# A grouped 1x1 convolution that streams through SBUF: input and output rings of four slots each, in place of three and five

## The chip, the core and the metric

The kernel runs on one core of a Trainium2 chip. The core has five engines, each with its own instruction queue: TensorE (PE, matrix products; its weight loads are listed as PEld), VectorE (DVE), ScalarE (ACT), GpSimd (POOL) and SyncE (SP). They are synchronised by semaphores only. Sixteen DMA engines move data between the memory (HBM) and the on-chip buffer (SBUF, 128 partitions); matrix products land in PSUM. Transfers are issued here by SP, ACT and GpSimd, and each of the three has its own DMA queue on every DMA engine.

The metric is the device time of one execution in microseconds (us), the median over several runs. A profile is one further execution with an instruction and DMA trace; its times are its own.

## The reference

The input `x` is 1 x 512 x 512 x 192 in bf16, the weights `w` are 1 x 1 x 4 x 48 x 48. The 192 channels of each pixel form four groups of 48, and each group is multiplied by its own 48 x 48 matrix:

```
xg  = x.reshape(B, H, W, 4, 48)
out = einsum('bhwgc,gcd->bhwgd', xg, w[0, 0]).reshape(B, H, W, 192)
```

There are 262,144 pixels of 384 bytes: 100.66 MB to read and as much to write.

## The kernel before

**Pieces and slots.** The pixels are cut into pieces (`plan_pieces`, L78). A full piece has 64 columns (`SLOT`): 128 partitions, each with 64 consecutive pixels, 24,576 bytes per partition and 3.1 MB in all. There are 34 slots in order, numbered from 0. Slot 0 is loaded as three pieces of 8, 24 and 32 columns (`HEAD`). Slots 6 and 22 (`SHARED_AT`) are shared ones: they hold data in part of the partitions only, partitions 0 to 15 with 48 columns, moved by SP's queue (by ACT's when stored), and partitions 52 to 95 with 64 columns, moved by GpSimd's queue. With them the DMA engines get unequal shares. The last slot has 8 columns.

**Rings.** `xin` and `xout` are rings in SBUF. The input ring has `IN_COLS` = 192 columns, three slots; the output ring has `OUT_COLS` = 320 columns, five slots. A slot's place in a ring is its column modulo the ring's size.

**Groups and pairs.** Four columns make a group (16 groups in a slot), two groups a pair. For each pair PE transposes twelve 128 x 128 blocks of `xin` into PSUM (`transposes`, L260), DVE copies them to SBUF as bf16 (`evacuate`, L311), PE multiplies the twelve blocks by a banded weight matrix `wt` (`matmuls`, L275), and ACT copies each group's result from PSUM to `xout` (L345). PE works one pair ahead with the transposes.

**Loops.** PE's code is a loop whose body is as long as the input ring: `LOOP` = `IN_COLS // 4` = 48 groups, `LP` = 24 pairs. There are 265 pairs: 11 turns of the loop and one pair behind it. DVE loops over the same number of pairs. ACT, SP and GpSimd have straight code.

**What sets the order.** Each engine's list is written out by hand.
- SP (L228) waits before each load until the slot's room in the ring is free (`groups_before`, L179: PE has transposed the slot that was there before), and then issues the load.
- GpSimd (L184) goes through the pieces. For each it first looks at the piece after it; if that is a shared one, it waits for the room and issues GpSimd's part of that load. Then it waits until piece `p` has landed and raises `ready` (L218), on which PE waits. After that it issues GpSimd's part of a shared store, if the piece before was a shared one. Small dummy transfers (`cur`, L203) turn the round-robin over the DMA engines to the wanted one.
- ACT (L323) waits before a group's copy until the store of the slot that was in that place of the output ring has landed (`wait_stored`, L333), then for PE, then copies. A slot's store is issued after the second group of the next slot (L346). The last eight full slots are stored in halves of 32 columns, and the very last of them in four parts (`LATE`, `LAST_PARTS`).

Of the kernel before, what the change touches and what calls it, by code (L numbers as in the profile page):

```python
# [22 lines left out]
ECOLS = 272  # L23

SLOT = 64
IN_COLS = 3 * SLOT
OUT_COLS = 5 * SLOT
HEAD = (8, 24, 32)
LATE = 9
LAST_PARTS = (24, 16, 12, 12)  # L30
LOOP = IN_COLS // 4
SHARED_AT = (6, 22)
SYNC, POOL = 0, 1
SHARED = ((0, 16, 4, 48, SYNC), (52, 44, 11, SLOT, POOL))
NXP = 4
NXS = 2
NOB = 4
# [22 lines left out]
class Piece:  # L60

    def __init__(self, i, slot, g0, size, shares, pix):
        self.i, self.slot, self.size = i, slot, size
        self.at = {IN_COLS: 4 * g0 % IN_COLS, OUT_COLS: 4 * g0 % OUT_COLS}
        self.g0, self.g1 = g0, g0 + size // 4
# [12 lines left out]
def plan_pieces(npix):  # L78
    few = sum(rows * cols for _, rows, _, cols, _ in SHARED)
    at = list(SHARED_AT)  # L80
    if npix < len(at) * few + 128 * SLOT * (1 + at[-1]):
        at = []
    cols = (npix - few * len(at)) // 128
    assert cols % 4 == 0
    pieces, g, pix, n = [], 0, 0, 0
    while cols:
        if n in at:
            parts = [(SLOT, SHARED)]
        elif n == 0 and cols >= SLOT:
            parts = [(s, None) for s in HEAD]  # L90
        else:
            parts = [(min(SLOT, cols), None)]
        for s, shares in parts:
            pieces.append(Piece(len(pieces), n, g, s, shares, pix))
            cols -= 0 if shares else s
            g, pix = pieces[-1].g1, pieces[-1].pix_end
        n += 1
    assert pix == npix
    return pieces


def bass_standalone__grouped__vision_kernel(nc, x, w, out):
# [5 lines left out]
    pieces = plan_pieces(npix)  # L108
# [11 lines left out]
    def groups(pair):  # L120
        return range(2 * pair, min(2 * pair + 2, NG))

    def transfers(ap, ring, p, queue, c0=0, c1=None):
        at = p.at[ring.shape[1] // C]
        for b in p.on(queue):
            px = ap[b.pix:b.pix + b.rows * b.cols, :]
            e0, e1 = c0, min(c1 or b.cols, b.cols)
            if b.parts == 1:
                view = px.rearrange("(p i) n -> p (i n)", p=b.rows)[:, e0 * C:e1 * C]
            else:  # L130
                view = px.rearrange("(c a i) n -> a c (i n)", a=b.parts, c=b.rows // b.parts)
            yield b, view, ring[b.r0:b.r0 + b.rows, (at + e0) * C:(at + e1) * C]

    stores = []
    for p in pieces:
# [6 lines left out]
        for n in parts:  # L142
            stores.append((p, c, c + n, p.g0 + (c + n) // 4))
            c += n
    store_of = {g: i for i, (p, c0, _, g1) in enumerate(stores) for g in range(p.g0 + c0 // 4, g1)}
    pooled = [p for p in pieces if p.on(POOL)]
    pool_val = {p: 16 * len(p.on(POOL)) for p in pooled}

    with ExitStack() as es:
        block = es.enter_context(nc.Block())  # L150
        xin = es.enter_context(nc.sbuf_tensor("xin", [128, IN_COLS * C], BF16))
        xout = es.enter_context(nc.sbuf_tensor("xout", [128, OUT_COLS * C], BF16))
        xT_sb = [es.enter_context(nc.sbuf_tensor(f"xT_sb{i}", [128, 4 * UC], BF16)) for i in range(NXS)]
# [3 lines left out]
        wt = es.enter_context(nc.sbuf_tensor("wt", [128, WCOLS], BF16))  # L157
        xT_ps = es.enter_context(nc.psum_tensor("xT_ps", [128, NXP, 1024], BF16))
        o_ps = es.enter_context(nc.psum_tensor("o_ps", [128, NOB, 512], F32))
# [19 lines left out]
        def groups_before(p):  # L179
            pairs = (p.g1 - LOOP + 1) // 2  # L180
            return max(2 * pairs - 3, pairs > 0)

        @block.gpsimd
        def _(gp):  # L184
            wq = Waiter(gp)
            gp.memset(esel[:], 1.0).then_inc(p0_sem, 1)  # L186
            gp.memset(ident[:], 1.0).then_inc(p1_sem, 1)  # L187
            gp.wait_ge(p0_sem, 1)
            gp.affine_select(out=esel[:], in_=esel[:], pattern=[[-1, ECOLS]],  # L189
                             compare_op=AluOpType.is_equal, fill=0.0, base=ESHIFT,  # L190
                             channel_multiplier=1).then_inc(e_sem, 1)
            gp.wait_ge(p1_sem, 1)
            gp.affine_select(out=ident[:], in_=ident[:], pattern=[[-1, 128]],  # L193
                             compare_op=AluOpType.is_equal, fill=0.0, base=0,
                             channel_multiplier=1).then_inc(id_sem, 1)
            cursor, turns = [0], [0]

            def pool_dmas(p, ap, ring, inward, done):
                for b, dram, sbuf in transfers(ap, ring, p, POOL):
                    turn = (b.engine - cursor[0]) % 16  # L200
                    if turn:
                        few = xf[0:turn, 0:128].rearrange("p (a b) -> p a b", a=2)[:, :, 0:32]
                        gp.dma_start(cur[0:turn, turns[0]], few).then_inc(cur_sem, 16)  # L203
                        turns[0] += 1
                    gp.dma_start(*((sbuf, dram) if inward else (dram, sbuf))).then_inc(done, 16)  # L205
                    cursor[0] = (b.engine + b.parts) % 16

            for p in pieces:
                ahead = pieces[p.i + 1] if p.i + 1 < len(pieces) else None
                if ahead in pooled:  # L210
                    wq.wait(mm_done, groups_before(ahead))
                    pool_dmas(ahead, xf, xin, True, pl_sem[ahead])
                wq.wait(ld_sem[p.i], 16 * len(p.on(SYNC)))
                if p in pooled:
                    wq.wait(pl_sem[p], pool_val[p])
                pairs = (NP if p is pieces[-1] else p.g1 // 2) - p.g0 // 2
                if pairs:
                    gp.sem_inc(ready, pairs)  # L218
                if p.i and pieces[p.i - 1] in pooled:
                    q = pieces[p.i - 1]  # L220
                    wq.wait(mm_done, q.g1 + 2)
                    pool_dmas(q, of, xout, False, ps_sem[q])
            for p in pooled:
                wq.wait(ps_sem[p], pool_val[p])
            wq.wait(cur_sem, 16 * turns[0])

        @block.sync
        def _(sp):  # L228
            wq = Waiter(sp)
            sp.dma_start(w_sb[:], wv).then_inc(w_sem, 16)  # L230
            for p in pieces:
                wq.wait(mm_done, groups_before(p))
                for _, dram, sbuf in transfers(xf, xin, p, SYNC):
                    sp.dma_start(sbuf, dram).then_inc(ld_sem[p.i], 16)  # L234

        @block.tensor
        def _(pe):
# [12 lines left out]
            def transposes(j, gs):  # L250
# [4 lines left out]
                for g in gs:  # L255
                    xg = columns(xin, g)
                    for ul in range(2):
                        for tc in range(3):
                            i = ul * 3 + tc
                            last = pe.transpose(xT_ps[:, g % NXP, i * 128:(i + 1) * 128],  # L260
                                                xg[:, i * 128:(i + 1) * 128], ident[:])
# [40 lines left out]
        def _(dve):  # L302
# [4 lines left out]
            def evacuate(pair, j):  # L307
                n = len(groups(pair))
                b0 = pair * 2 % NXP
                dve.wait_ge(t_left, j + 1)  # L310
# [12 lines left out]
        def _(act):  # L323
# [3 lines left out]
            def store():  # L327
                i = len(stores) - len(todo)
                p, c0, c1, g1 = todo.pop(0)
                for _, dram, sbuf in transfers(of, xout, p, SYNC, c0, c1):  # L330
                    act.dma_start(dram, sbuf).then_inc(st_sem[i], 16)  # L331

            def wait_stored(i):  # L333
                p = stores[i][0]
                wq.wait(st_sem[i], 16 * len(p.on(SYNC)))
                if p in pooled:
                    wq.wait(ps_sem[p], pool_val[p])

            for g in range(NG):
                if g >= OUT_COLS // 4:  # L340
                    wait_stored(store_of[g - OUT_COLS // 4])
                wq.wait(mm_done, g + 1)
# [38 lines left out]
```

## Time and profile before

| | us |
|---|---|
| median of three runs (480.93 to 483.29) | 481.1 |
| profiled execution | 480.09 |
| its span, first to last instruction | 478.35 |
| PE busy | 439.6 |
| ACT busy | 399.1 |
| DVE busy | 254.4 |

The profile counts 201.48 MB over the DMA queues, a mean of 421 GB/s over the span: SP's queue (loads, q1) takes 48.5% of the sixteen DMA engines' time, ACT's queue (stores, q10) 48.4%, GpSimd's (q0) 2.1%. The granted clock of TensorE was full except for 6.8 us from 310.1 us on.

How to read it: an engine's busy share is a mean over the whole span, and a wait is put down to the instruction that released it. "POOLq L218" is GpSimd's forwarding of a landed load, so a wait of PE for it is a wait for a load. "DMA share" is the mean busy share of the sixteen DMA engines in a stretch. A transfer's time to landing runs from its issue to the last of its parts.

### The profile page before, as it was taken

To read this page: it belongs to the slowest core of one execution; us is meant where nothing else is said; L and a number is where in the kernel's file an instruction comes from. 1 tells how busy PE (TensorE), PEld (TensorE's weight loads), DVE (VectorE), ACT (ScalarE), POOL (GpSimd) and SP (SyncE) were. 2 spreads that over 40 slices of the span, in tenths; PEclk is the share of its full clock that TensorE was granted. 3 is DMA by queue.
4 is the path that set the end of the run, shared out by engine and by line. 5 is a ranking of instruction groups with operands and counts; after the bars stand their busy time and mean duration, and the time that the engine had idled before them with its cause. 6 is when DMAs were issued, how large, how long until landed. Compare 5 with 4: busy or idle time off the path is not lost.

```text
span 478.4 us, 14098 instructions
## 1 busy us (share of the span) xinstructions
PE 439.6 (92%) x6370; PEld 395.4 (83%) x6370; DVE 254.4 (53%) x266; ACT 399.1 (83%) x531; POOL 5.9 (1%) x16
## 2 busy tenths in 40 slices
PE   5999999999999998888998888799999999999990
PEld 5989888889888897777887777788889889888880
DVE  2565555555555555545555454356555555555640
ACT  2899899899899987887978878499899989989990
POOL 1000010000000000000000000000000000000000
PEclk9999999999999999999999999799999999999996
DMA  8999999999999999999999999999999999999995
GB/s 330 427 405 438 427 430 417 427 430 438 427 434 430 430 432 432 432 430 436 432 428 430 434 432 433 435 430 423 430 418 427 428 430 424 424 418 422 429 426 247
DMA packets 11978, 201.48 MB, mean 421 GB/s; under 512 B 1744, under 2 KB 1744, under 8 KB 2640
## 3 DMA queue, kind: packets, MB, share of 16 engines
q1 hardware_dynamic: 5144, 98.52, 48.5%
q10 hardware_dynamic: 6376, 98.50, 48.4%
q0 software_dynamic: 448, 4.33, 2.1%
q8 instruction: 5, 0.08, 0.1%
q14 instruction: 5, 0.04, 0.0%
HBM read 100.68 MB, written 100.66 MB: 421 GB/s over the span
## 4 chain that ended last, share of the span: by engine, by line
PE 69%; DMA 27%; issue 1%; ACT 0%; SPq 0%; ACTq 0%; POOLq 0%
PE o_ps L275 40%; PE xT_ps L260 29%; DMA xin<-in_x_dram 27%; ACT xout L345 0%; SPq L234 0%; SPq L230 0%; POOLq L218 0%; ACTq L331 0%; ACTq L50 0%
## 5 line engine op out<-in xcount | busy, mean ns | idle before, releaser
L345 ACT CAST xout<-o_ps 128x768 bf16<-128x768 f32 x530 | 397.8, 802 | 67.1 <-PE o_ps L275 56.3
L311 DVE COPY xT_sb<-xT_ps 128x1536 bf16<-128x1536 bf16 x265 | 253.8, 958 | 206.6 <-PE xT_ps L260 206.6
L275 PE MATMUL o_ps<-wt,xT_sb 128*128 128x144 bf16 (+1 forms) x3180 | 296.3, 235 | 3.5 <-ACT xout L345 0.4
L275 PEld LDWEIGHTS o_ps<-wt,xT_sb 128*128 128x128 bf16 x3180 | 214.7, 98 | 43.8 <-ACT xout L345 29.8
L260 PE MATMUL xT_ps<-ident,xin 128*128 128x128 bf16 x3180 | 224.1, 221 | 20.1 <-POOLq L218 18.6
L260 PEld LDWEIGHTS xT_ps<-ident,xin 128*128 128x128 bf16 x3180 | 192.4, 99 | 23.7 <-POOLq L218 21.0
L203 POOL DMA_DIRECT2D cur<-in_x_dram x4 | 2.3, 584 | 328.3 <-DMA xin<-in_x_dram 178.9
L246 PE MATMUL o_ps<-w_sb,esel 48*128 48x48 bf16 x10 | 0.6, 210 | 2.8 <-DMA w_sb<-in_w_dram 2.8
L246 PEld LDWEIGHTS o_ps<-w_sb,esel 48*128 48x128 bf16 x10 | 0.5, 113 | 2.8 <-issue 2.8
L305 DVE CAST wt<-o_ps 128x480 bf16<-128x480 f32 x1 | 0.7, 657 | 3.4 <-PE o_ps L246 3.4
L345 ACT ACT_TABLE_LOAD x1 | 1.3, 1283 | 0.8 <-PEq L366 0.8
L205 POOL DMA_DIRECT2D xin<-in_x_dram x2 | 1.1, 563 | 0.0
L205 POOL DMA_DIRECT2D out_dram<-xout x2 | 1.1, 560 | 0.0
L189 POOL TENSOR_SCALAR_AFFINE_SELECT esel<-esel 48x272 bf16<-48x272 bf16 x1 | 0.4, 402 | 0.0
L186 POOL MEMSET esel<- 48x272 bf16 x1 | 0.3, 318 | 0.3 <-POOLq L366 0.3
L193 POOL TENSOR_SCALAR_AFFINE_SELECT ident<-ident 128x128 bf16<-128x128 bf16 x1 | 0.3, 282 | 0.0
L187 POOL MEMSET ident<- 128x128 bf16 x1 | 0.2, 198 | 0.0
L366 POOL MEMSET const-float32-0.0<- 128x1 f32 x1 | 0.1, 98 | 0.3 <-issue 0.3
L366 POOL MEMSET const-bfloat16-1.0<- 128x1 bf16 x1 | 0.1, 101 | 0.0
L366 POOL MEMSET const-uint8-127<- 128x1 uint8 x1 | 0.1, 101 | 0.0
L366 POOL MEMSET const-float32-1.0<- 128x1 f32 x1 | 0.1, 99 | 0.0
## 6 DMA issues: line engine op xcount, KB each, us to landing
xin<-in_x_dram SPq DMA_DIRECT2D x30, 3072.0 KB, 22.2
out_dram<-xout ACTq DMA_DIRECT2D x22, 3072.0 KB, 25.1
out_dram<-xout ACTq DMA_DIRECT2D x15, 1536.0 KB, 27.5
out_dram<-xout ACTq DMA_DIRECT2D x2, 1152.0 KB, 16.7
xin<-in_x_dram POOLq DMA_DIRECT2D x2, 1056.0 KB, 15.9
out_dram<-xout POOLq DMA_DIRECT2D x2, 1056.0 KB, 16.3
xin<-in_x_dram SPq DMA_DIRECT2D x1, 1536.0 KB, 8.9
xin<-in_x_dram SPq DMA_DIRECT2D x1, 1152.0 KB, 5.7
```

The lines of the kernel that those rows point to most:

```text
L186: gp.memset(esel[:], 1.0).then_inc(p0_sem, 1)
L189: gp.affine_select(out=esel[:], in_=esel[:], pattern=[[-1, ECOLS]], compare_op=AluOpType.is_equal, fill=0.0, base=ESHIFT, channel_multipli ...
L193: gp.affine_select(out=ident[:], in_=ident[:], pattern=[[-1, 128]], compare_op=AluOpType.is_equal, fill=0.0, base=0, channel_multiplier=1) ...
L203: gp.dma_start(cur[0:turn, turns[0]], few).then_inc(cur_sem, 16)
L205: gp.dma_start(*((sbuf, dram) if inward else (dram, sbuf))).then_inc(done, 16)
L246: last = pe.matmul(o_ps[:, NOB - 1, col:col + CG], lhsT=esel[:, s0:s0 + 128], rhs=w_sb[:, g, :], start=True, stop=True, skip_group_check=True)
L260: last = pe.transpose(xT_ps[:, g % NXP, i * 128:(i + 1) * 128], xg[:, i * 128:(i + 1) * 128], ident[:])
L275: last = pe.matmul(o_ps[:, v % NOB, c0_:c1_], lhsT=xs[:, i * 128:(i + 1) * 128], rhs=wt[:, WOFF[tc]:WOFF[tc] + (c1_ - c0_)], start=(tc == ...
L305: dve.tensor_copy(wt[:], o_ps[:, NOB - 1, 0:WCOLS]).then_inc(wc_sem, 1)
L311: dve.tensor_copy(xT_sb[pair % NXS][:, 0:n * 2 * UC].rearrange("p (g c) -> p g c", g=n), xT_ps[:, b0:b0 + n, 0:2 * UC]).then_inc(e_left, 1)
L345: act.copy(dst, o_ps[:, v % NOB:v % NOB + 2, 0:UC]).then_inc(o_left, 1)
L366: nc = _bacc.Bacc("TRN2", target_bir_lowering=False, num_devices=1)
```

## The change

Both rings get 256 columns, four slots each; together they take the same room as before. Since PE's and DVE's loops are as long as the input ring, their bodies grow from 24 to 32 pairs: 8 turns, and nine pairs behind them. A load of slot k may be issued once slot k-4 is done; ACT's copy into slot k waits for the store of slot k-4. In its list GpSimd looks two pieces ahead for a shared load, not one: a new constant, `AHEAD`, is the number of input slots less two.

```diff
 SLOT = 64
-IN_COLS = 3 * SLOT
-OUT_COLS = 5 * SLOT
+IN_COLS = 4 * SLOT
+OUT_COLS = 4 * SLOT
 HEAD = (8, 24, 32)
...
 SHARED = ((0, 16, 4, 48, SYNC), (52, 44, 11, SLOT, POOL))
+AHEAD = IN_COLS // SLOT - 2
...
             for p in pieces:
-                ahead = pieces[p.i + 1] if p.i + 1 < len(pieces) else None
+                ahead = pieces[p.i + AHEAD] if p.i + AHEAD < len(pieces) else None
                 if ahead in pooled:
                     wq.wait(mm_done, groups_before(ahead))
                     pool_dmas(ahead, xf, xin, True, pl_sem[ahead])
```

## The prediction

> **What bounds the kernel now.** I read the share of each engine first, then the stages, then the waits, then the DMA issues, and last the end of the time line. Page and stages (columns: stretch, its length, then busy time and count for PE, PEld, DVE, ACT, POOL, then clock, DMA share, GB/s):
>
> ```profile
> span 478.4 us, 14098 instructions
> PE 439.6 (92%) x6370; PEld 395.4 (83%) x6370; DVE 254.4 (53%) x266; ACT 399.1 (83%) x531; POOL 5.9 (1%) x16
> PE 69%; DMA 27%; issue 1%; ACT 0%; SPq 0%; ACTq 0%; POOLq 0%
> q8 instruction: 5, 0.08, 0.1%
> ...
> 12.00:60.00 48.00, 47.63 (x698) 42.97 (x696) 27.65 (x29) 43.26 (x58) 0.00 (x0) 1.00 1.01 424
> 76.00:140.00 64.00, 63.04 (x927) 56.59 (x925) 36.77 (x39) 57.61 (x77) 1.10 (x2) 1.00 1.00 429
> 166.00:296.00 130.00, 118.62 (x1730) 105.84 (x1728) 68.86 (x73) 107.84 (x145) 1.10 (x2) 1.00 1.00 432
> 366.00:445.00 79.00, 77.66 (x1146) 70.07 (x1144) 45.75 (x48) 71.41 (x96) 0.00 (x0) 1.00 1.00 425
> 445.00:470.00 25.00, 20.41 (x295) 17.95 (x292) 11.49 (x12) 20.11 (x27) 0.00 (x0) 1.00 1.00 425
> 470.00:478.40 8.40, 0.00 (x0) 0.00 (x0) 0.00 (x0) 0.00 (x0) 0.00 (x0) 0.51 0.42 174
> ```
>
> The chain names PE, but see the DMA share: 1.00 in every stage from 12 to 470 us. All sixteen DMA engines work without a gap, in both directions, and 201.48 MB at 432 GB/s is 466 us by itself. PE is second: it is idle only in the stretch 166 to 296 (118.6 of 130), where it waits for loads. The next lines are the waits, the DMA issues and the end of the time line:
>
> ```profile
> ACT xout L345 <- PE o_ps L275: 56.3, 131, 7.7
> PE xT_ps L260 <- POOLq L218: 18.6, 12, 4.9
> ...
> xin<-in_x_dram SPq DMA_DIRECT2D x30, 3072.0 KB, 22.2
> out_dram<-xout ACTq DMA_DIRECT2D x22, 3072.0 KB, 25.1
> out_dram<-xout ACTq DMA_DIRECT2D x15, 1536.0 KB, 27.5
> ...
> DMA to landing us min/median/max: 10.8/24.6/35.4
> ...
> 301.79 1.46 PE L260 MATMUL xT_ps<-ident,xin 128*128 128x128 bf16 x12 [4.87 <-POOLq L218]
> 466.18 0.80 ACT L345 CAST xout<-o_ps 128x768 bf16<-128x768 f32 x1
> 467.01 0.68 ACTq L331 DMA_DIRECT2D out_dram<-xout  x1
> ```
>
> "PE <- POOLq L218" is PE waiting for a load (GpSimd forwards each landing): 18.6 us in all. ACT never waits for a store, so five output slots are not all needed. The last line is the key to the end: the last store is issued at 467.0, and its sixteen parts land between 472.5 and 477.85. PE and ACT are done 10.8 us before the end; what ends the run is the queue of stores, and in it the most loaded of the sixteen engines.
>
> **The change, part by part.** The sum is made against the profiled execution: 480.09 us, of which 478.35 is the span and 1.74 lies around it. The median of the runs shown, 481.1, is 1.0 above that.
>
> *Loads one slot further ahead.* SP issues the load of slot k when PE has finished slot k-4, not k-3, about one slot (13.1 us at PE's own pace, 14.55 us from 180 to 282, by the spacing of SP's issues) earlier. This gives work to an engine only if its load queue would be empty. From the issue and landing times, transfer by transfer, that is so in one place of weight: slot 5 lands from 65.1 us on, slot 7 is issued at 73.5, and slot 6 is the shared one, so for about 9 us most engines had stores alone. Elsewhere the next load is issued before the last has landed, but for at most 3 us (slot 23 from 313.9, slot 24 issued 316.6). In those gaps the engines were not idle: they worked on stores (share 1.00). The loads so gained cost as much store work. Saving in DMA time: 0. Gain for PE: at equal turns 4.5 us of work moved puts later loads up to 9 us earlier and later stores up to 9 us later; for engines that also had the shared slot in between it is less. I take 6.
>
> *Output ring of four slots.* A whole slot's store is issued after the second group of the next slot and its room is needed at slot k+4's first group: 46 groups of 0.82 us (13.1/16) = 37.7 us, where it was 62 groups, 50.8 us. Half-slot stores near the end have 54 groups, 44.3 us. Landing takes 28.2 us (median from 166 to 296) and 35.4 at most. With stores 6 us later, and issued earlier because PE is earlier, ACT will now wait for stores. Behind that wait on ACT stand its copies and the issue of later stores; PE waits for the copies through four PSUM buffers. What is late next can be read off absolute times: slot 20 begins now when its load lands, at 283.6. In the changed kernel it needs that load (277 to 281) and the store of slot 16 (272.2 now, 278 to 281 then). So PE starts slot 20 some 3 us earlier, held by a store in place of a load. PE's idle time falls from 18.6 us to about 15, between 0 and 34 (bounds: no wait at all; the slowest engine's store pace of 15.1 us per slot, 242.04 to 257.18 to 272.24, holding PE for slots 16 to 33: 17 x 2.0 us). On the path: 0, because DMA keeps its queues filled and PE ends before the stores do.
>
> *GpSimd two pieces ahead.* Its load of slot 6 goes out when slot 2 is done (47.0 us; now 61.4), that of slot 22 when slot 18 is done (about 267; now 284.8). Each sits before GpSimd's release of the slot then due: slot 4 lands at 51.7 and PE needs it at 60.5; slot 20 lands about 280. Neither release is late. Each puts a third queue beside two, four packets of 0.91 us on each of eleven engines. Now that collides with slot 21's load (34.4 us to landing, the longest) and makes the 4.9 us wait at 301.8; the clock is halved for 6.8 us from 310.1 behind it. Moved one slot, it collides with slot 20's instead, or is absorbed. PE idle -8 to +5 us; off the path, 0. SP's own share of the slot moves alike, and GpSimd's cursor DMAs stay four.
>
> *A longer loop.* PE's loop has 32 pairs, not 24; one turn is 1181 instructions in the trace and will be about 1575; 8 turns and 9 pairs behind them. A turn of the loop costs PE some 0.3 us (the 0.2 to 0.5 us before L260 marked issue), so three fewer save 1 us, off the path. Code: five packets of 16 KB, at 17 to 52 us, all in the first turn and each on another engine, 0.94 us each; the longer code needs two to four more. Take 3 x 0.94 / 16 = 0.2 us; bounds 0 and 2.8 (all on the engine that ends last).
>
> *DMA rate.* Stages ran at 424 to 432 GB/s. If the 130 us at 432 fell to 425, +2.1; if the 152 us from 318 to 470 rose to 432, -2.5. No reason for either: 0.
>
> *The end.* With loads ahead, they finish earlier (now 444) and a longer stretch is stores alone. At that point PE still has some 35 us of work and the engines some 45 us of stores (7.3 us per slot: 8 packets of 0.912), so they don't run dry. The last engine's total of bytes is unchanged: 0.
>
> Sum: 480.09 + 0.2 = 480.3; on the median's scale 481.3.
>
> **The rivals.**
> *Slower: the store wait outgrows the reserve behind PE.* Place: ACT's wait for a store before its copy. PE may lose 10.8 - 3.4 = 7.4 us net (3.4 us: the first 384 KB load, the nearest row for a last transfer that meets no queue) before the end moves; then each us costs one. If the pace of 15.1 held from slot 12 to 31, idle is 19 x 2.0 = 38, less the 18.6 and 3.4 us (half of 6.8) of now: +16. Then 467 + 16 + 3.4 = 486.4 span, 489. Against: when PE is held, loads are held too, and the stores catch up. 0.16.
>
> *Slower: the loop's code no longer stays on chip.* A miss at each branch back: 0.94 us behind two packets of 0.91, 2.8 us, 7 times: 19 us; PE at 486, span 490, time 492. For: the body grows by a third. [...] 0.05.
>
> *Slower: DMA works less evenly.* The last engine falls another 2 us behind and the rate falls by the 2.1 us above: 485. 0.09.
>
> *Faster: the load wait was the bound.* A deeper ring takes away the 18.6 us: 462. Against: share 1.00; the bytes alone need 466. 0.02. [...]
>
> *Faster: the engines end closer together.* The mean of the sixteen last landings is 474.0, the last is 477.85. Closing most of it, with the later rate at 432: 476 to 477. 0.16.
>
> **How the numbers follow.** About 0.5% (2.4 us) is what a measurement of this kernel can tell. My case, no change, 0.52, its own range 479 to 483.5. Slower 0.16 + 0.05 + 0.09 = 0.30; faster 0.18. The range 477 to 488 leaves out half of the first slow rival and the second, the 462, and part of the even ending: nearly 2 in 10.
>
> **What would show it.** Right: DMA share 1.00 from 12 to 470; "ACT xout <- DMA out_dram" waits appear, 5 to 15 us in all; PE's waits for L218 fall below 10; seven to nine code packets; last copy at 461 to 470. Wrong: a DMA share under 0.97 in any stage between, a last copy after 475, or code packets in every turn.

## The result: 0.7% faster

Nine runs of the changed kernel have a median of 477.42 us, nine of the kernel before 481.1. The ratio of the means is 0.993, with a 95% interval of 0.9902 to 0.9959. The profiled execution took 477.15 us, its span is 475.2, 3.1 us less than before. The time lies just inside the range that was given (477 to 488), but the forecast was "no change", at 481.3, with 0.18 for faster. It came closest to the last of the rivals: "the engines end closer together", 476 to 477.

The page of the changed kernel, and its stages (columns as in the prediction):

```profile
span 475.2 us, 14075 instructions
PE 437.6 (92%) x6370; PEld 394.6 (83%) x6370; DVE 254.5 (54%) x266; ACT 399.0 (84%) x531; POOL 5.9 (1%) x16
PE 75%; DMA 20%; issue 1%; ACT 0%; SPq 0%; ACTq 0%; POOLq 0%
q8 instruction: 8, 0.13, 0.1%
...
12.00:60.00 48.00, 47.47 (x707) 43.04 (x705) 27.84 (x30) 44.12 (x60) 1.26 (x2) 1.00 1.01 422
76.00:140.00 64.00, 63.11 (x934) 57.06 (x931) 37.05 (x40) 58.32 (x78) 1.11 (x2) 1.00 1.00 431
166.00:296.00 130.00, 118.70 (x1705) 106.66 (x1703) 67.99 (x71) 106.58 (x143) 1.11 (x2) 0.97 1.01 432
366.00:445.00 79.00, 77.79 (x1147) 70.08 (x1145) 45.44 (x48) 71.91 (x96) 0.00 (x0) 1.00 1.00 428
445.00:470.00 25.00, 13.61 (x194) 11.80 (x191) 7.66 (x8) 13.55 (x19) 0.00 (x0) 0.81 0.99 419
470.00:475.20 5.20, 0.00 (x0) 0.00 (x0) 0.00 (x0) 0.00 (x0) 0.00 (x0) 0.50 0.43 177
```

The DMA share is 1.00 again, up to the last stretches. The rate is not the same: 431 for 429 GB/s from 76 to 140, 428 for 425 from 366 to 445. A share of 1.00 says that a packet is under way all the time, not that packets take their usual time.

Waits, DMA issues, and the end:

```profile
ACT xout L346 <- PE o_ps L276: 51.5, 134, 7.6
PE xT_ps L261 <- POOLq L219: 13.1, 8, 4.9
ACT xout L346 <- DMA out_dram<-xout: 0.3, 1, 0.3
...
xin<-in_x_dram SPq DMA_DIRECT2D x30, 3072.0 KB, 35.6
out_dram<-xout ACTq DMA_DIRECT2D x22, 3072.0 KB, 32.3
...
459.30 0.80 ACT L346 CAST xout<-o_ps 128x768 bf16<-128x768 f32 x1
460.13 0.47 ACTq L332 DMA_DIRECT2D out_dram<-xout  x1
```

PE and ACT are done 6.9 us earlier than before, and the last store takes 14.6 us to land, not 10.8: as in the kernel before, the stores end the run. Loads take 35.6 us from issue to landing, not 22.2: they are issued earlier, and stand longer in a queue that stays filled.

**Where the 3.1 us came from.** The sixteen parts of the last store land at a mean of 472.3 us (before 473.9), the last of them at 474.7 (before 477.85). So 1.6 us is in the mean of the engines, and 1.5 us in how far the last one is behind the mean. For the mean, I added up per engine what each packet took beyond its usual time (912 ns for 24 KB, 460 for 12 KB, and so on): 4.5 us before, 2.8 with the change. The code packets cost 0.2 us more, as forecast. After 55 us there are 101 packets that overrun by over 0.1 us before, and 8 with the change.

**Where the last engine lost it.** In a stage with full queues a packet starts within 4 ns of the end of the one before on its engine, so the engines can be followed one by one. One of them is slow throughout: it needs 15.1 us for a slot's load and store where the others need 14.5, in both kernels. It is the one engine that carries nothing of the shared slots (GpSimd's 24 KB packets, four an engine, run on eleven of the others, the 18 KB packets on the remaining four), and it ends last all the same. In the kernel before it met this, from 66 to 77 us and from 77 to 84 (first the queues, then the stages; kernel before):

```profile
q10 hardware_dynamic: 140, 3.05, 72.1%
q0 software_dynamic: 80, 0.98, 23.0%
q1 hardware_dynamic: 18, 0.27, 6.3%
...
66.00:77.00 11.00, 10.89 (x165) 9.93 (x163) 6.36 (x7) 9.94 (x15) 0.00 (x0) 1.00 1.03 435
77.00:84.00 7.00, 6.96 (x106) 6.25 (x103) 4.17 (x5) 6.41 (x9) 0.00 (x0) 1.00 0.96 400
```

and the same with the change:

```profile
q10 hardware_dynamic: 100, 2.33, 54.4%
q1 hardware_dynamic: 100, 2.02, 46.9%
...
66.00:77.00 11.00, 10.93 (x165) 9.98 (x164) 6.30 (x8) 10.09 (x14) 0.00 (x0) 1.00 1.01 433
77.00:84.00 7.00, 6.89 (x103) 6.10 (x101) 4.25 (x5) 6.41 (x10) 0.00 (x0) 1.00 0.98 421
```

(The queue lines are of 67 to 77 us.) Before, SP's load queue (q1) has 6% of the engines' time: it has run dry, as the prediction said. Then slot 7's load is issued at 73.5, its first packets run from 76.9 us on, on most engines by 77.9, and there the rate falls to 400 GB/s for 7 us. The packets that overrun come before the engine's first load: stores of 24 KB that take 1.48, 1.30, 1.67 and 1.86 us in place of 0.91 to 1.0 on the slow engine, whose first load starts only at 80.2, and one store each of 1.7 to 1.8 us on three others. The first of the four runs at 71.1 us, while the load queue is empty and before slot 7's load is issued; the other three run after its issue. From 65.0 to 82.9 us the slow engine moved 16 packets; with the change it moved 19 in the same time (one of them not in the records). That is 2.7 us of work, on the engine that ends the run.

### The profile page after: what moved, and what is told of

It reads as the page before. It is cut to its first block, busy times and chain, and to the rows that moved or that the text cites. A ratio compares the mean times of both kernels' runs of the same rounds, so it can differ in the third digit from the quotient of the medians.

```text
span 475.2 us, 14075 instructions
## 1 busy us (share of the span) xinstructions
PE 437.6 (92%) x6370; PEld 394.6 (83%) x6370; DVE 254.5 (54%) x266; ACT 399.0 (84%) x531; POOL 5.9 (1%) x16
## 4 chain that ended last, share of the span: by engine, by line
PE 75%; DMA 20%; issue 1%; ACT 0%; SPq 0%; ACTq 0%; POOLq 0%
PE o_ps L276 43%; PE xT_ps L261 31%; DMA xin<-in_x_dram 20%; ACT xout L346 0%; SPq L235 0%; SPq L231 0%; ACTq L332 0%; POOLq L219 0%; ACTq L51 0%
## 5 line engine op out<-in xcount | busy, mean ns | idle before, releaser
L261 PE MATMUL xT_ps<-ident,xin 128*128 128x128 bf16 x3180 | 223.4, 220 | 14.4 <-POOLq L219 13.1
L261 PEld LDWEIGHTS xT_ps<-ident,xin 128*128 128x128 bf16 x3180 | 192.0, 99 | 17.4 <-POOLq L219 14.7
## 6 DMA issues: line engine op xcount, KB each, us to landing
xin<-in_x_dram SPq DMA_DIRECT2D x30, 3072.0 KB, 35.6
out_dram<-xout ACTq DMA_DIRECT2D x2, 1152.0 KB, 18.6
```

## The experiments

Theory 1: what costs is a load queue that runs dry and is started again; the change helps because loads are queued a slot earlier. Theory 2: the gain comes from the layout of the rings or the longer loop. A third: from GpSimd's earlier loads. Each ratio is to runs of the kernel before, on the same chip. In the table, "overruns" are the store packets over 0.1 us too long between 64 and 84 us, and "last, next" the landings of the last store on the last engine and the one before it, in the profiled execution.

| run | ratio to before, 95% | overruns 64 to 84 | last, next us |
|---|---|---|---|
| before | 1 | 8 | 477.9, 476.0 |
| the change | 0.993 (0.9902 to 0.9959) | 0 | 474.7, 473.8 |
| e1: loads as late as with three slots | 1.0007 (0.9989 to 1.0024) | 10 | 477.2, 474.2 |
| e2: three input, four output slots | 0.9994 (0.9978 to 1.0009) | 10 | 478.6, 476.8 |
| e3: GpSimd one piece ahead | 0.9928 (0.9907 to 0.9948) | 0 | 475.0, 473.8 |
| e4: late loads from slot 23 | 0.9932 (0.9912 to 0.9953) | 0 | 474.9, 474.9 |
| e5: late loads up to slot 8 | 0.9983 (0.9964 to 1.0002) | 10 | 477.1, 474.1 |
| e6: late loads, slots 9 to 22 | 0.9976 (0.9944 to 1.0009) | 2 | 476.8, 475.8 |
| e7: two dry spells | 0.9962 (0.9942 to 0.9981) | 0 | 476.3, 475.1 |

**e1, when the loads are issued.**

```diff
-AHEAD = IN_COLS // SLOT - 2
+AHEAD = 1
+LEAD = 3 * SLOT // 4
...
-            pairs = (p.g1 - LOOP + 1) // 2
+            pairs = (p.g1 - LEAD + 1) // 2
```

> The changed kernel's rings and loops (4 and 4 slots, 32 pairs), but every load is issued no earlier than with three input slots (SP and GpSimd wait for slot k-3, GpSimd looks one piece ahead). Theory 1 (a load queue that runs dry makes DMA packets overrun their usual time; the change helps because loads are queued a slot earlier): the time goes back to that of before, ratio 0.998 to 1.004, and DMA packets that take over 100 ns longer than usual after 60 us come back, some 100 against 7 with the change. Theory 2 (the gain comes from the rings' layout, the equal rings or the longer loop, not from when loads are issued): ratio 0.993 as with the change, few overrunning packets.

Rings, loops and code are those of the change, and the gain is gone. Theory 2 has fallen. The overruns are back at 64 to 84 us, but fewer than expected in all (42 after 55 us, not 100): the many of the kernel before after 310 us did not come back, and the time is that of before all the same.

**e2, the smaller output ring alone.**

```diff
-IN_COLS = 4 * SLOT
+IN_COLS = 3 * SLOT
 OUT_COLS = 4 * SLOT
```

> Input ring back to three slots (loop of 24 pairs, GpSimd one piece ahead), output ring four slots: the smaller output ring alone. Theory 1: the output ring costs nothing by itself, ratio 0.998 to 1.004, some 100 overrunning packets, ACT waits for stores under 2 us in all. Theory 2, in the form that the equal rings bring the gain: 0.993. A third view, that the smaller output ring costs time which the input ring more than pays back: ratio above 1.005.

No difference to before: the fifth output slot had not been needed, and giving it up neither costs nor brings anything.

**e3, GpSimd's part.**

```diff
-AHEAD = IN_COLS // SLOT - 2
+AHEAD = 1
```

> The changed kernel with GpSimd looking one piece ahead, as before; SP's loads are issued as with the change. Theory 1: nearly all of the gain stays, ratio 0.992 to 0.996, since GpSimd issues only two of the loads; overrunning packets under 20. If GpSimd's part is what counts: ratio 0.998 or more.

The whole gain stays. Looking two pieces ahead does nothing that shows.

**e4, the late loads.** With e4 I meant to bring back the overruns after 310 us, which were the most by number.

```diff
-            pairs = (p.g1 - LOOP + 1) // 2
+            pairs = (p.g1 - (LEAD if p.slot >= GATED else LOOP) + 1) // 2
```

(`LEAD` is 48 groups, `GATED` 23.)

> The changed kernel, but loads of slot 23 and later are issued no earlier than with three input slots; before that as with the change. Theory 1: the overrunning packets come back after about 310 us only (some 80), and with them most of the gain goes: 1.4 us of the 3.1 us in the mean end of the DMA engines and probably the part of the last engine, ratio 0.996 to 1.000. Theory 2: 0.993, few such packets.

It missed: the gain stays, and the overruns did not come back (7 after 310 us). Yet the load queue did run dry, and was started again. Slot 21 lands from 288.2 us on, slot 23 is issued only at 297.4. The queues of e4 from 294 to 300 us:

```profile
q10 hardware_dynamic: 115, 2.58, 100.3%
q1 hardware_dynamic: 16, 0.04, 1.8%
```

The slow engine has no load from 291.9 to 301.8 us, the others for 5.5 to 9.1 us. No packet overruns there or behind it up to 315 us, and the last engine lands at 474.9, within 0.2 us of the change. So a load queue that runs dry and is started again need not cost anything: theory 1 as it is worded does not hold. The same profile has 17 loads that overrun between 124 and 129 us, by 4.9 us together, with the load queue filled and no order changed yet; they cost the last engine nothing that shows. So overruns also come without a dry queue, and what counts is which engine has them. The loss had to be earlier; the first place where the load queue is dry is at 65 to 77 us.

**e5 and e6, where.**

```diff
-            pairs = (p.g1 - LOOP + 1) // 2
+            pairs = (p.g1 - (LEAD if p.slot <= 8 else LOOP) + 1) // 2
```

(`AHEAD` is 1; e6 has `9 <= p.slot <= 22` in place of `p.slot <= 8`.)

> The changed kernel with GpSimd one piece ahead; loads up to slot 8 are issued no earlier than with three input slots, all later ones as with the change. Theory 1 in its new form (what costs is a load queue that ran dry and is started again; in the kernel before that happens first at about 65 to 80 us, around the shared slot 6, and there the slowest of the sixteen DMA engines loses some 3 us, three others 0.8 us each): most of the loss is back with this one spell, ratio 0.997 to 1.001, five engines with overrunning packets between 60 and 84 us. Rival (the loss builds up in the long middle, where PE waits for each load): 0.993.

> The counterpart: only the loads of slots 9 to 22 are held to the time of three input slots, those before and after are as with the change; GpSimd one piece ahead. Theory 1: no engine's load queue runs dry at 65 us, the gain stays, ratio 0.991 to 0.996. Rival (the middle is where it is lost): 0.997 or more.

e5 is the run that shows where. Against e3 only the loads of slots 3 to 8 are later (slots 0 to 2 wait in neither), the orders behind them are the same, and the ratio is 0.9983 in place of 0.9928: within 0.2% of before. The queues from 67 to 77 us, e5:

```profile
q10 hardware_dynamic: 141, 3.07, 73.8%
q0 software_dynamic: 74, 0.98, 23.0%
q1 hardware_dynamic: 14, 0.19, 4.5%
```

They are those of the kernel before. The last engine lands at 477.1, the next at 474.1: one engine is 3.0 us behind, and after 84 us only 19 packets overrun anywhere in this run. The mean of the sixteen, 472.9, is 0.6 us behind that of the change, the last engine 2.4: what counts is the one engine, not the mean.

e6 was made badly. Holding slot 9 for a slot makes a dry spell of its own: slot 8 lands from 95.2 on, slot 9 is issued at 102.2 and starts late, and 33 packets overrun between 84 and 140 us, by 12.9 us together. So it is no counterpart to e5. As the expectations stood, theory 1 missed (0.991 to 0.996) and the rival's 0.997 or more was met. The interval, 0.9944 to 1.0009, reaches into that of the change, and the overruns lie behind the spell at 95 to 105 us; so the run fits a spell moved by some 30 us, but it doesn't rule out the rival.

**e7, dry spells where there were none.** Slots 12 and 17 wait for the slot two before them.

```diff
-            pairs = (p.g1 - LOOP + 1) // 2
+            pairs = (p.g1 - (LEAD if p.slot in LATER else LOOP) + 1) // 2
```

(`LEAD` is 32 groups, `LATER` is (12, 17).)

> The changed kernel with two dry spells made on purpose: the loads of slots 12 and 17 (and so the next one) wait until the slot two before them is done, at about 152 and 217 us, when the loads ahead of them have landed on most engines. DMA still has stores to work on. Theory 1: each spell costs the slowest engine 1 to 3 us; ratio to before 0.996 to 1.004, overrunning packets at about 153 to 160 us and at the second spell if it goes dry. If dryness costs nothing as long as stores are queued: 0.993.

The queues of e7 from 146 to 156 us:

```profile
q10 hardware_dynamic: 189, 4.13, 96.3%
q1 hardware_dynamic: 5, 0.12, 4.6%
```

The load queue is dry, stores have 96%, the mean rate is 426 GB/s, and behind it 23 packets overrun from 154 to 163 us, all of them loads. The second spell, at 217 to 228, is milder (q1 has 25%). Against the change (0.993, and 0.9928 when it was run again) the two cost about 0.3%, some 1.5 us, near the lower end of what was expected; the intervals overlap a little. GpSimd's queue and the shared slots have no part in these spells, so, as far as this difference holds, a spell can cost without the third queue. Whether the third queue adds to the loss at 65 us, where it has 23%, is not tested; the spell of e4, which cost nothing, was without it. In e7 mostly loads overrun, in e5 stores; why, I don't know.

**e9 and e10, the two slow rivals.** e9 has an output ring of three slots, e10 five input and three output slots, with a loop of 40 pairs.

```diff
-OUT_COLS = 4 * SLOT
+OUT_COLS = 3 * SLOT
```

(e10 has also `IN_COLS = 5 * SLOT` and `AHEAD = 2`.)

> Input ring of four slots, output ring of only three: does the output ring hold PE back, and does that cost time? A slot's store then has 30 groups or 24.6 us from its issue until its room is needed, and with the change stores take 32 us (median). ACT must wait for stores in most slots. The slow rival of the prediction (the store wait ends PE later than the stores): ratio 1.01 or more. The prediction's own view (when PE is held, loads are held too, stores catch up, DMA stays full until the reserve behind PE is used up): 0.993 to 1.005, DMA share 1.00 until PE's last copy, the last copy some 8 to 15 us later than with the change.

> [...] The rival of the code (a body that no longer stays on chip): code packets of 16 KB in every later turn, against eight in all with the change, and PE stalls at the turns. If it still stays: ten to thirteen such packets in all. Against the run with four and three slots, theory 1 (depth beyond what keeps the load queue fed gives nothing) says the same time within 0.3%.

e9: ratio 1.0033 (1.0005 to 1.0061), 482.66 us. Its waits and its end:

```profile
ACT xout L346 <- DMA out_dram<-xout: 28.2, 14, 5.3
PE o_ps L276 <- ACT xout L346: 22.0, 14, 4.6
...
445.00:470.00 25.00, 24.64 (x367) 22.23 (x365) 14.36 (x15) 22.44 (x32) 0.00 (x0) 1.00 0.89 375
...
476.40 0.81 ACT L346 CAST xout<-o_ps 128x768 bf16<-128x768 f32 x1
477.24 0.34 ACTq L332 DMA_DIRECT2D out_dram<-xout  x1
```

With three slots the wait for stores is there, and it goes on to PE. PE's last work falls so late that the DMA share drops to 0.89 before 470, and all sixteen engines land their last part within 1.2 us, at 479.9 to 481.0. The prediction's own view had the share at 1.00 until PE's last copy; that missed. The end has passed from the stores to PE. Its last copy is 17 us later than with the change (15 was the expected upper end), and the run costs 5 us against it: the change had 477.62 us beside it (e11). Four output slots are just enough here.

e10: ratio 1.0417 (1.0353 to 1.048), 501 us. Its page:

```profile
PE xT_ps L261 <- issue: 26.6, 5, 7.2
...
q8 instruction: 58, 0.95, 0.7%
```

Against eight code packets with the change there are 58, in every turn of the loop, and PE stands still at each of the five returns to the loop's start, up to 7.2 us and 26.6 us in all, waiting for nothing that the profile shows. The rival of the code is real, a size further on: with a loop of 32 pairs (some 1575 instructions) the later turns fetch nothing (the eight packets run up to 61.2 us and from 450.7 us on, none in between), with one of 40 pairs (some 1970 at the same count for a pair) every turn fetches. Where between the two the limit lies, no run shows. e9, with three output slots too, took 482.66 us, so the output ring is not what makes e10 slow. Theory 1's expectation for this run can't be read: the refetch hides it.

**e11 and e12 (and e8), a try for a better version.** With the change three engines land at 468.6 to 468.8, 5 us before most. e8 gives the first partitions of the shared slots more columns:

```diff
-SHARED = ((0, 16, 4, 48, SYNC), (52, 44, 11, SLOT, POOL))
+SHARED = ((0, 16, 4, SLOT, SYNC), (52, 44, 11, SLOT, POOL))
```

> A try for a better version: the changed kernel, but in the shared slots the first 16 partitions hold 64 columns, not 48, so the piece behind slot 32 shrinks from 8 to 4 columns on all engines. With the change three engines end at 468.6, most at 473.4 to 473.8, the last at 474.7. If the three early ones are among the four that serve those partitions, the others shed 4 columns of load and store, 0.9 us, and the early ones gain 2.7: ratio 0.990 to 0.992. If not, 0.993 or up to 0.998.

> The changed kernel unaltered, beside the next run on the same chip, to compare the two: ratio to before 0.991 to 0.996, no engine with overrunning packets at 60 to 84 us.

> The version with 64 columns in the first 16 partitions of the shared slots, once more: its span was 0.9 us shorter in the profiles, as worked out, but its interval overlapped that of the change. If the gain is real: its median 0.3 to 1.0 us below that of the changed kernel in this call, ratio 0.990 to 0.993.

e8: 477.0 us, 0.9924 (0.9897 to 0.9952), its profile 473.8 for the last engine and 471.0 for the first, as worked out. Run again, the change itself had 477.62 us, 0.9928 (0.9882 to 0.9974) (e11), and beside it e12, the same kernel as e8, 477.47, 0.9913 (0.9878 to 0.9947); its last engine landed at 476.2 in the profile this time. The early engines are moved for certain; a gain in time beyond the change is not shown.

## Why the prediction was wrong

- *What bounds the kernel, and what ends it.* Right in the main: DMA share, the end by the queue of stores, PE as second. Two readings were wrong. The last engine is not "the most loaded of the sixteen": it alone carries nothing of the shared slots, and it is last because it is slow (15.1 against 14.5 us per slot). And PE was idle not only from 166 to 296 us, but also from 296 to 318 (busy 17.0 of 22), where the wait of 4.9 us lies.
- *"Loads one slot further ahead ... Saving in DMA time: 0."* This is the step that failed. The dry spell at 65 to 75 us was found, and its price was set to nothing since "the engines were not idle: they worked on stores (share 1.00)". Busy was taken for as fast as ever. In and behind this spell packets overran: 2.7 us on the slow engine, which ends the run, and 0.8 to 0.9 us on three others. e1, e3 and e5 show that this spell carries most of the gain: the ratio goes from 0.9928 to 0.9983 when the loads of slots 3 to 8 alone are late. For the other dry spells a price of nothing was not always wrong: that of e4 at 294 to 300 us cost nothing.
- *"DMA rate ... No reason for either: 0."* Mis-sized: from 318 to 366 us the rate went from 426 to 431 GB/s, from 366 to 445 from 425 to 428. The overruns of the kernel before after 310 us (82 packets, 20 us over all engines) belong here. e1 and e5 are without most of them and still near the time of before, so they are not what counted.
- *"The end ... The last engine's total of bytes is unchanged: 0."* The bytes are; its time is not. The last engine went from 3.9 us behind the mean to 2.4.
- *Output ring.* ACT's waits were forecast at 5 to 15 us, and are 0.3. I shifted all stores by 6 us. The store of slot 16 lands last at 272.8, where 272.2 was before: its last part is that of the slow engine, which had won 2.7 us, while the first part moved from 266.0 to 268.9. The load of slot 20 landed at 281.5, half a us after the 277 to 281 given. e9 bounds the rest: the mechanism of this rival is right, and it decides at three slots, not four.
- *PE.* Its wait for loads fell from 18.6 to 13.1 us; about 15 was said of all its idle time, but "below 10" among the signs of being right, and that missed. The last copy started at 459.3, a little before the 461 to 470 given. Off the path, as said.
- *GpSimd.* 0 said, 0 found (e3). PE's wait of 4.9 us moved to the load of slot 20, which took 49.0 us to land; that was one of the two cases given. The half clock lies beside this wait, not behind it at 310.1 us: the granted clock is 0.51 from 299.4 to 306.4 us in the kernel before, 0.50 from 280.0 to 286.7 with the change. *Longer loop.* 0.2 us said; 0.2 found, with eight code packets of the seven to nine.
- *Rivals.* "The load wait was the bound" (462) falls, though PE's waits for loads do go with the time from e1 to e5 (18.0, 18.5, 12.4, 14.7 and 20.6 us): the last store is issued 10.8 us before the end in the kernel before and 14.6 with the change, and the engines work on stores from there on. The end is theirs. The even ending was given 0.16 with its price about right (476 to 477, measured 477.4), but without its mechanism, as something that might happen; with this spell priced, it would have been the forecast. That the time lies inside the range, by 0.4 us, is luck.

## What to carry to other kernels

A DMA share of 1.00 is no proof of a full rate (here it stood at 1.00 with 425 GB/s and with 432): look at the GB/s of the same stretch, at packets that take longer than their usual time, and at which queue is empty there. Where loads and stores share saturated engines, a load queue that runs dry can cost time even while stores keep the engines busy (2.7 us on the slow engine here, nothing in e4), so don't price it at nothing: try one slot more in the ring, and look at the engine that ends last. When the transfers end the run, follow the slowest engine, not the mean; and count a loop's instructions before a ring makes it longer (here some 1575 were fetched once, some 1970 in every turn).

## What the runs showed of the hardware

- One DMA engine is 4% slower than the others throughout, in both kernels: 15.1 against 14.5 us per slot of loads and stores, with 24 KB packets of 0.91 to 1.0 us where the others take 0.91. What slows it is not in the trace.
- With both queues filled, load and store packets ran in strict turn, the 4-byte packets at the end of a part counted: from 180 to 230 us on the fourteen engines that can be followed through in either kernel (61 to 63 packets each), and on the slow engine of the changed kernel from 72.7 to 83 us.
- Beside a filled store queue, a load queue that was empty from about 65 to 77 us cost 2.7 us on the slow engine, 0.8 to 0.9 us on three others and nothing on the rest; one that was empty from about 294 to 301 us (e4) cost nothing on any.
- A loop body of PE of some 1970 instructions is fetched again in every turn (58 code packets, e10), at up to 7.2 us of standstill for each; one of some 1575 is not (eight).

What stays open: why packets overrun at one dry spell and not at another, why the slow engine loses most at 65 to 80 us, and why it is stores in one case and loads in another. The length of the spell may count (the slow engine was without loads for 16 us in the kernel before, for 10 in e4), and so may GpSimd's queue, which is busy in the one and not in the other. e7 speaks for the length: its first spell, 13 to 17 us on the engines, had no part of GpSimd's queue, and packets overran behind it; no run tests it by itself. Whether the dryness or the restart is the cause was not separated either: one of the slow engine's four overruns began before the load was issued, three after.
